# Splitting float64 weights with one ScalarE pass and no GpSimd work in a two-stage token network

## The chip, the core and the metric

The kernel runs on one core of a Trainium2 chip. Five engines take part, each with its own queue, worked off in order: TensorE (PE, with PEld for its weight loads), VectorE (DVE), ScalarE (ACT), GpSimd (POOL) and SyncE (SP), which issues most transfers. The metric is device time in microseconds (us) of one execution; the median of three timed executions of the kernel before is 1495.04 us (1490.94 to 1497.68).

## What is computed

The reference chains three parts. Only the last two carry float64 weights that the change touches.

```
x   = attention(q, k pooled by 8, v pooled by 8)          # 8 x 576 tokens, 512 wide
x   = moe(x)            # 8 experts, each token goes to one: relu(x @ w1[e]) @ w2[e], times a gate
h   = x @ w_in                                            # 4608 x 512 by 512 x 2048
g   = h * clip(h + 3, 0, 6) / 6
out = g @ w_out                                           # 4608 x 2048 by 2048 x 512
```

`w_in` and `w_out` come in as float64. The chip's engines work with 32 bits, so the kernel reads each float64 as two 32-bit words and makes two float32 numbers of it, a high part (what TensorE takes in its float32r format) and a low part (the rest). Activations are split into a high and a low part too. Each product is then three matmuls: high by high, low by high, high by low.

## The kernel before

It runs in three stages. **Attention** builds the tokens and writes them, ordered by expert, to memory. **moe1** works in units of 400 tokens of one expert; beside its matmuls each unit of its loop loads and splits a piece of `w_in` (two pieces of 128 by 416 values, by `conv` inside `moe1`, all on VectorE). **moe2** is the last stage: 9 blocks of 512 tokens, and in each block 16 steps, one for each 128 columns of the 2048 wide middle layer. Step s does

- `h_mm(s)`: 12 matmuls into `hps` (128 by 512); ScalarE makes r = relu(hps + 3); VectorE makes r = min(r, 6) * hps; ScalarE rounds it to `gh`; the low part is `gl` = r - gh.
- `o_mm(s - 2)`: 12 matmuls of `gh` and `gl` with the high and low part `wo` of one 128 by 512 tile of `w_out`, added up over the 16 steps in four PSUM tiles.

In the first block alone, step s begins with `conv(s)`, which makes the `wo` tiles of that step from the loaded tile `ds` (32-bit words, high and low word side by side), and then `conv_load(s + 2)` asks for the `ds` tile of the step after next. After steps 3, 6, 9 and 12 `y_split` also splits a tile of the next block's input: a copy on ScalarE (`yhl`, high) and a difference on VectorE (`yhl`, low). I call these four the split steps.

The order on TensorE, VectorE, ScalarE and SyncE is the order in which the code is written. On VectorE, step s of the first block is: the seven operations of `conv(s)` (lines 989 to 995), r (line 1016), and, in a split step, the low part of `yhl` (line 745). On ScalarE it is: the high part `wo[0]` (line 997, needs line 993), r (line 1015), `gh` (line 1019, needs line 1016), in a split step the high part of `yhl`. On GpSimd it is: the difference a - high (line 998), the sum that gives the low part `wo[1]` (line 999), and, in the first block alone, `gl` (line 1020); later blocks make `gl` on VectorE. TensorE cannot begin the matmuls of `o_mm(s)` with `wo[1]` before line 999 is done, nor those with `gl` before line 1020 is.

The seven VectorE operations of `conv` are: clear the sign of the high word (989), a floor (990), shift by 3 and mask (991), put the sign back (992), flip one exponent bit to get the float32 a (993), cut a's mantissa off to get a power of two, ex (994), low word times ex (995).

Of the kernel before, what the change touches and what calls it, by code (L numbers as in the profile page):

```python
# [8 lines left out]
F32 = mybir.dt.float32  # L9
F32R = mybir.dt.float32r  # L10
BF16 = mybir.dt.bfloat16
I32 = mybir.dt.int32
U32 = mybir.dt.uint32
AF = mybir.ActivationFunctionType
ALU = mybir.AluOpType
# [36 lines left out]
F64_MIN = 2.0 ** -15 * 1.125  # L52
# [6 lines left out]
def setup(tc, g, cp):  # L59
    nc = tc.nc  # L60
    g.idn = cp.tile([P, P], F32, name="idn")
    make_identity(nc, g.idn)
    g.three = cp.tile([P, 1], F32, name="three")
    nc.vector.memset(g.three, 3.0)
    g.sgn = cp.tile([P, 1], I32, name="sgn")
    nc.vector.memset(g.sgn, -2 ** 31)


def attention(tc, g, moe, ins, xr_d):
# [675 lines left out]
    nc.vector.tensor_tensor(lo, src, hi.bitcast(F32), op=ALU.subtract)  # L745


def moe1(tc, g, xr_d, tok_d, y_d, w1, w2, w_in):
    nc = tc.nc
    s = Ctx()  # L750
# [89 lines left out]
    def conv(t, c, h):  # L840
        sh = [P, 2, CW]
        hw = t[:, :, :, 1]
        u, a, m, ex = (s.cv.tile(sh, I32, name=n, tag=n) for n in ("u", "a", "m", "ex"))
        oh = g.wi[0][:, 2 * h:2 * h + 2, bass.ds(c, CW)]
        ol = g.wi[1][:, 2 * h:2 * h + 2, bass.ds(c, CW)]
        v = nc.vector
        af = a.bitcast(F32)
        return [
            lambda: v.tensor_scalar(u, hw, 0x7FFFFFFF, None, op0=ALU.bitwise_and),
            lambda: v.tensor_scalar(m.bitcast(F32), u.bitcast(F32), F64_MIN, None, op0=ALU.max),  # L850
            lambda: v.tensor_scalar(u, m, 3, 0x7FFFFFFF, op0=ALU.logical_shift_left, op1=ALU.bitwise_and),
            lambda: v.scalar_tensor_tensor(m, hw, g.sgn, u, op0=ALU.bitwise_and, op1=ALU.bitwise_or),
            lambda: v.tensor_scalar(a, m, 0x40000000, None, op0=ALU.bitwise_xor),
            lambda: v.tensor_scalar(ex, m, -0x800000, 0x40000000, op0=ALU.bitwise_and, op1=ALU.bitwise_xor),
            lambda: v.scalar_tensor_tensor(u.bitcast(F32), t[:, :, :, 0].bitcast(U32), 2.0 ** -52, ex.bitcast(F32),
                                           op0=ALU.mult, op1=ALU.mult),
            lambda: v.tensor_scalar(oh, af, 1.0, None, op0=ALU.mult),
            lambda: v.tensor_tensor(m.bitcast(F32), af, oh.bitcast(F32), op=ALU.subtract),
            lambda: v.tensor_tensor(ol, m.bitcast(F32), u.bitcast(F32), op=ALU.add),
        ]  # L860

    def unit(i, first=False, last=False, tail=None):
        e = s.e0 if first else reg(0, i, E - 1)
# [98 lines left out]
def moe2(tc, g, tok_d, y_d, w_out, out):  # L962
    nc = tc.nc
    es = ExitStack()
    pool = lambda n, b, **kw: es.enter_context(tc.tile_pool(name=n, bufs=b, reuse_waits="tile", **kw))
    c1 = pool("dc", 1)
    gp = pool("dg", 3)
    op = pool("do", 3)
    cv = pool("dcv", 1)
    ps_h = pool("ps_h", 3, space=PSUM)  # L970
    ps_o = pool("ps_o", 1, space=PSUM)
    NB = NT // 512
    KF = F2 // P
    wo = [[c1.tile([P, DM], F32R, name=f"wo{h}_{f}") for f in reversed(range(KF))][::-1] for h in (1, 0)][::-1]
    three, sgn = g.three, g.sgn
    yhl, y_load, y_split = g.yhl, g.y_load, g.y_split

    sts, conv_load = g.sts, g.wo_load

    def conv(f):  # L980
        s = sts.pop(f)
        sh = [P, DM]
        hw = s[:, :, 1]
        u = cv.tile(sh, I32, name="du", tag="u")
        a = cv.tile(sh, I32, name="da", tag="a")
        m = cv.tile(sh, I32, name="dm", tag="m")
        ex = cv.tile(sh, I32, name="dex", tag="ex")
        v = nc.vector
        v.tensor_scalar(u, hw, 0x7FFFFFFF, None, op0=ALU.bitwise_and)  # L989
        v.tensor_scalar(m.bitcast(F32), u.bitcast(F32), F64_MIN, None, op0=ALU.max)  # L990
        v.tensor_scalar(u, m, 3, 0x7FFFFFFF, op0=ALU.logical_shift_left, op1=ALU.bitwise_and)  # L991
        v.scalar_tensor_tensor(m, hw, sgn, u, op0=ALU.bitwise_and, op1=ALU.bitwise_or)  # L992
        v.tensor_scalar(a, m, 0x40000000, None, op0=ALU.bitwise_xor)  # L993
        v.tensor_scalar(ex, m, -0x800000, 0x40000000, op0=ALU.bitwise_and, op1=ALU.bitwise_xor)
        v.scalar_tensor_tensor(wo[1][f], s[:, :, 0].bitcast(U32), 2.0 ** -52, ex.bitcast(F32), op0=ALU.mult, op1=ALU.mult)
        af = a.bitcast(F32)
        nc.scalar.copy(wo[0][f], af)
        nc.gpsimd.tensor_tensor(ex.bitcast(F32), af, wo[0][f].bitcast(F32), op=ALU.subtract)
        nc.gpsimd.tensor_tensor(wo[1][f], ex.bitcast(F32), wo[1][f].bitcast(F32), op=ALU.add)  # L999

    tkf = c1.tile([P, NT // P], F32, name="tkf")
    tki = c1.tile([P, NT // P], I32, name="tki")
    gg = {}

    def h_mm(s):
        j, f = divmod(s, KF)
        yh, yl = yhl[j]
        ps = ps_h.tile([P, 512], F32, name="hps", tag="h")
        n = 0
        for k in range(4):  # L1010
            for a, b in ((0, yh), (0, yl), (1, yh)):
                nc.tensor.matmul(ps, g.wi[a][:, k, f * P:(f + 1) * P], b[:, k], start=(n == 0), stop=(n == 11))  # L1012
                n += 1
        r = gp.tile([P, 512], F32, name="r", tag="r", bufs=2)
        nc.scalar.activation(r, ps, AF.Relu, bias=three)  # L1015
        nc.vector.scalar_tensor_tensor(r, r, 6.0, ps, op0=ALU.min, op1=ALU.mult)  # L1016
        gh = gp.tile([P, 512], F32R, name="gh", tag="gh")
        gl = gp.tile([P, 512], F32R, name="gl", tag="gl")
        nc.scalar.copy(gh, r)  # L1019
        (nc.gpsimd if s < KF else nc.vector).tensor_tensor(gl, r, gh.bitcast(F32), op=ALU.subtract)  # L1020
        gg[s] = (gh, gl)

    pso = {}

    def put(j, t):
        o = op.tile([P, DM], F32, name="osb", tag="osb")
        if t % 2:
            nc.vector.tensor_scalar(o, pso[j][t], 1.0 / 6.0, None, op0=ALU.mult)
        else:
            nc.scalar.activation(o, pso[j][t], AF.Copy, scale=1.0 / 6.0)  # L1030
# [45 lines left out]
def chunk_kernel(ctx, tc, q, k, v, mid, w_gate, mbias, w1, w2, w_in, w_out, out):  # L1076
# [76 lines left out]
```

## Time and profile before

| | us |
|---|---|
| median of three timed runs | 1495.04 (1490.94 to 1497.68) |
| the profiled execution, its own time | 1481.43 |
| span of its trace, first to last instruction | 1479.7 |
| PE busy / DVE busy / ACT busy / POOL busy | 1426.0 / 793.7 / 533.6 / 259.3 |

The profile gives the busy time of each engine, the share of each in slices of the span, the chain of work that ended last, and groups of instructions. PE's busy share is high nearly everywhere, since its matmuls overlap and their ends are modelled, so whether it waits is read from the matmuls' idle times and from their count in a stretch. Attention takes the first 208 us, moe1 goes to 648.8 us of the trace, and moe2 fills the rest; its first block, in which the weights are split, lies between 649 and 767 us.

### The profile page before, as it was taken

How to read it: one execution, taken by the hardware profiler on the slowest of the kernel's cores; microseconds unless marked ns; L12 is line 12 of the kernel's file. 1: busy time of each engine (PE TensorE's matmuls, PEld its weight loads, DVE VectorE, ACT ScalarE, POOL GpSimd, SP SyncE). 2: the span in 40 equal slices, each digit the busy share in tenths (PEclk: the TensorE clock that was granted, in tenths of full speed). 3: DMA queues.
4: the chain of work that ended last, by engine and by line, in shares of the span. 5: the costliest groups of instructions: out<-in, count | busy, mean ns of one | idle time of the engine just before them, and what ended most of it. 6: DMA issues, size and time to landing. Idle time of an engine off the chain costs nothing.

```text
span 1479.7 us, 22270 instructions
## 1 busy us (share of the span) xinstructions
PE 1426.0 (96%) x7385; PEld 1243.1 (84%) x7385; DVE 793.7 (54%) x1554; ACT 533.6 (36%) x1057; POOL 259.3 (18%) x265
## 2 busy tenths in 40 slices
PE   7998989999999999998889999999999999999998
PEld 5787879999999999986668888888888888888886
DVE  7879875877777777668873232222223223232222
ACT  3556654444444444422232222222222222222222
POOL 5537231111111111025550010100001010010101
PEclk8999999999999999999999999999999999999999
DMA  8989155666666666452220010100101010000000
GB/s 271 295 282 325 67 167 177 203 190 186 190 186 187 195 186 191 130 145 78 86 86 15 15 38 20 36 15 8 43 15 36 15 36 15 15 29 0 29 1 29
DMA packets 128937, 156.57 MB, mean 106 GB/s; under 512 B 18466, under 2 KB 87074, under 8 KB 128866
## 3 DMA queue, kind: packets, MB, share of 16 engines
q1 hardware_dynamic: 123106, 135.54, 30.5%
q0 software_dynamic: 5760, 20.10, 3.6%
q8 instruction: 43, 0.70, 0.2%
q14 instruction: 28, 0.23, 0.1%
HBM read 118.26 MB, written 37.34 MB: 105 GB/s over the span
## 4 chain that ended last, share of the span: by engine, by line
issue 41%; PE 8%; DVE 6%; POOL 2%; ACT 1%; POOLq 0%; DVEq 0%; ACTq 0%
PE ops L1040 3%; PE hps L1012 3%; POOL out_dram L1031 2%; DVE dm L990 1%; PE ph L874 1%; DVE du L991 1%; PE y L887 1%; DVE du L989 1%; DVE dm L992 1%; ACT r L1015 1%; DVE r L1016 1%; DVE da L993 0%; DVE yhl L745 0%; ACT gh L1019 0%; ACT yhl L744 0%
## 5 line engine op out<-in xcount | busy, mean ns | idle before, releaser
L1012 PE MATMUL hps<-yhl,wi 128*128 128x512 f32 x1728 | 419.3, 391 | 0.0
L1012 PEld LDWEIGHTS hps<-yhl,wi 128*128 128x128 f32 x1728 | 325.3, 188 | 73.0
L1040 PE MATMUL ops<-wo,gh 128*128 128x512 f32 x1152 | 366.8, 398 | 3.4 <-POOL wo L999 3.4
L1016 DVE SCALAR_TENSOR_TENSOR r<-r,hps 128x512 f32<-128x512 f32 x144 | 98.9, 686 | 397.8 <-ACT r L1015 397.7
L1040 PEld LDWEIGHTS ops<-wo,gh 128*128 128x128 f32 x1152 | 217.7, 189 | 57.7 <-POOL wo L999 7.6
L1015 ACT ACTIVATE r<-hps,three 128x512 f32<-128x512 f32 x144 | 99.3, 690 | 415.6 <-PE hps L1012 415.0
L1040 PE MATMUL ops<-wo,gl 128*128 128x512 f32 x576 | 230.3, 400 | 12.8 <-POOL gl L1020 12.6
L745 DVE TENSOR_TENSOR wl<-ws,wh 128x512 fp32r<-128x512 f32 x192 | 136.2, 739 | 40.8 <-ACT wh L744 33.4
L744 ACT CAST wh<-ws 128x512 fp32r<-128x512 f32 x192 | 116.5, 619 | 106.3 <-PE y L887 55.4
L1031 POOL DMA_INDIRECT out_dram<-osb,tki x36 | 34.5, 959 | 674.6 <-ACT osb L1030 664.7
L1040 PEld LDWEIGHTS ops<-wo,gl 128*128 128x128 f32 x576 | 108.9, 189 | 43.0 <-POOL gl L1020 17.3
L1020 DVE TENSOR_TENSOR gl<-r,gh 128x512 fp32r<-128x512 f32 x128 | 88.9, 695 | 87.8 <-ACT gh L1019 87.8
L874 PE MATMUL ph<-xhi,wh 128*128 128x400 f32 x384 | 132.1, 344 | 2.2 <-PEq L1148 1.2
L887 PE MATMUL y<-hi,wh 128*128 128x400 f32 x384 | 133.9, 349 | 0.0
L887 PE MATMUL y<-lo,wh 128*128 128x400 f32 x384 | 132.4, 345 | 0.5 <-DVE lo L879 0.5
L874 PE MATMUL ph<-xlo,wh 128*128 128x400 f32 x384 | 132.6, 345 | 0.0
L874 PE MATMUL ph<-xhi,wl 128*128 128x400 f32 x384 | 132.6, 345 | 0.0
L887 PE MATMUL y<-hi,wl 128*128 128x400 f32 x384 | 131.4, 342 | 0.0
L1019 ACT CAST gh<-r 128x512 fp32r<-128x512 f32 x144 | 89.2, 620 | 109.7 <-DVE r L1016 109.7
L797 POOL TENSOR_TENSOR cxg<-cxg 100x512 f32<-100x512 f32 x48 | 57.7, 1205 | 331.4 <-PE ph L874 257.3
L878 ACT ACTIVATE hi<-ph 128x400 fp32r<-128x400 f32 x96 | 48.4, 504 | 106.4 <-PE ph L874 98.2
L879 DVE SCALAR_TENSOR_TENSOR lo<-ph,hi 128x400 fp32r<-128x400 f32 x96 | 54.9, 572 | 58.1 <-ACT hi L878 57.7
(194 smaller groups left out, 1692.0 us busy)
## 6 DMA issues: line engine op xcount, KB each, us to landing
ws<-in_moe_w_dram SPq DMA_DIRECT2D x192, 256.0 KB, 3.9
cxg<-xr SPq DMA_DIRECT2D x44, 225.8 KB
yd<-yo SPq DMA_DIRECT2D x12, 800.0 KB, 6.7
yt<-yd SPq DMA_DIRECT2D x36, 256.0 KB
cs<-in_moe_w_in_dram SPq DMA_DIRECT2D x20, 416.0 KB, 3.6
kv<-in_k_dram SPq DMA_DIRECT2D x16, 512.0 KB
kv<-in_v_dram SPq DMA_DIRECT2D x16, 512.0 KB
ds<-in_moe_w_out_dram SPq DMA_DIRECT2D x16, 512.0 KB
```

The source lines that it names most:

```text
L744: nc.scalar.copy(hi, src)
L745: nc.vector.tensor_tensor(lo, src, hi.bitcast(F32), op=ALU.subtract)
L797: nc.gpsimd.tensor_tensor(s.xg[:, t, 0:DM].rearrange("p (h x) -> p h x", x=D), v, s.xg[:, t, GC:GC + 1].unsqueeze(2).to_broadcast([T4, H, ...
L874: nc.tensor.matmul(ph, a[j][:, 0, k * P:(k + 1) * P], b[k], start=(n == 0), stop=(n == 11))
L887: nc.tensor.matmul(yps[d], a[j][:, 1, d * P:(d + 1) * P], b, start=(f == 0 and n == 0), stop=(f == 7 and n == 2))
L1012: nc.tensor.matmul(ps, g.wi[a][:, k, f * P:(f + 1) * P], b[:, k], start=(n == 0), stop=(n == 11))
L1015: nc.scalar.activation(r, ps, AF.Relu, bias=three)
L1016: nc.vector.scalar_tensor_tensor(r, r, 6.0, ps, op0=ALU.min, op1=ALU.mult)
L1019: nc.scalar.copy(gh, r)
L1020: (nc.gpsimd if s < KF else nc.vector).tensor_tensor(gl, r, gh.bitcast(F32), op=ALU.subtract)
L1031: i_ = nc.gpsimd.indirect_dma_start(out=out, out_offset=bass.IndirectOffsetOnAxis(ap=tki[:, 4 * j + t:4 * j + t + 1], axis=0), in_=o, in_o ...
L1040: nc.tensor.matmul(pso[j][t], a[:, t * P:(t + 1) * P], wo[b][f], start=(f == 0 and n == 0), stop=(f == KF - 1 and n == 2))
```

## The change

The split of a float64 tile becomes one function, `f64_ops`, used by both `conv` functions. It needs one operation less on integers: the sign is cleared by ScalarE's absolute value instead of a mask on VectorE, and the mask constant `sgn` now keeps the sign and one exponent bit, so that putting the sign back gives the float32 a at once and the bit flip goes away. In moe2 the two operations that GpSimd did (difference and sum) are VectorE's, and `gl` is VectorE's in the first block as in the others. In moe1 the high part stays on VectorE.

```diff
-    nc.vector.memset(g.sgn, -2 ** 31)
+    nc.vector.memset(g.sgn, -2 ** 30)

+def f64_ops(nc, g, hw, lw, a, m, ex, hi, lo, copy):
+    v = nc.vector
+    f = lambda t: t.bitcast(F32)
+    return [
+        lambda: nc.scalar.activation(f(ex), f(hw), AF.Abs),
+        lambda: v.tensor_scalar(f(m), f(ex), F64_MIN, None, op0=ALU.max),
+        lambda: v.tensor_scalar(m, m, 3, 0x3FFFFFFF, op0=ALU.logical_shift_left, op1=ALU.bitwise_and),
+        lambda: v.scalar_tensor_tensor(a, hw, g.sgn, m, op0=ALU.bitwise_and, op1=ALU.bitwise_or),
+        lambda: v.tensor_scalar(ex, a, -0x800000, None, op0=ALU.bitwise_and),
+        lambda: copy(hi, f(a)),
+        lambda: v.scalar_tensor_tensor(f(m), lw.bitcast(U32), 2.0 ** -52, f(ex), op0=ALU.mult, op1=ALU.mult),
+        lambda: v.tensor_tensor(f(ex), f(a), hi.bitcast(F32), op=ALU.subtract),
+        lambda: v.tensor_tensor(lo, f(ex), f(m), op=ALU.add),
+    ]
...
     def conv(f):
         s = sts.pop(f)
         sh = [P, DM]
         hw = s[:, :, 1]
...
-        v.scalar_tensor_tensor(wo[1][f], s[:, :, 0].bitcast(U32), 2.0 ** -52, ex.bitcast(F32), op0=ALU.mult, op1=ALU.mult)
-        af = a.bitcast(F32)
-        nc.scalar.copy(wo[0][f], af)
-        nc.gpsimd.tensor_tensor(ex.bitcast(F32), af, wo[0][f].bitcast(F32), op=ALU.subtract)
-        nc.gpsimd.tensor_tensor(wo[1][f], ex.bitcast(F32), wo[1][f].bitcast(F32), op=ALU.add)
+        a, m, ex = (cv.tile(sh, I32, name=f"d{n}", tag=n) for n in ("a", "m", "ex"))
+        for op_ in f64_ops(nc, g, hw, s[:, :, 0], a, m, ex, wo[0][f], wo[1][f], nc.scalar.copy):
+            op_()
...
-        (nc.gpsimd if s < KF else nc.vector).tensor_tensor(gl, r, gh.bitcast(F32), op=ALU.subtract)
+        nc.vector.tensor_tensor(gl, r, gh.bitcast(F32), op=ALU.subtract)
```

In `f64_ops` I name the operations by what they write, in order: abs, floor, shift, a, ex, high, m, difference, sum.

VectorE's queue in the first block of moe2, from r of step 3 to r of step 4, in the kernel before (`dm`, `da`, `dex`, `du` are the tiles m, a, ex and u of `conv`, and the brackets name the engines whose semaphores an instruction waits for):

```order
L1016 SCALAR_TENSOR_TENSOR r<-r,hps 128x512 [waits Activation_49]
L745 TENSOR_TENSOR yhl_4315<-yt,yhl_4314 128x512 [waits DMAHW0_49,Activation_49]
L989 TENSOR_SCALAR du<-ds 128x512 [waits DMAHW1_49]
L990 TENSOR_SCALAR dm<-du 128x512 [waits DVE_49]
L991 TENSOR_SCALAR du<-dm 128x512 [waits DVE_49]
L992 SCALAR_TENSOR_TENSOR dm<-ds,sgn,du 128x512 [waits DVE_49]
L993 TENSOR_SCALAR da<-dm 128x512 [waits DVE_49,Pool_49]
L994 TENSOR_SCALAR dex<-dm 128x512 [waits Pool_49]
L995 SCALAR_TENSOR_TENSOR wo_4_4128<-ds,dex 128x512 [waits DVE_49]
L1016 SCALAR_TENSOR_TENSOR r<-r,hps 128x512 [waits Activation_49]
```

The same stretch of VectorE's queue in the changed kernel:

```order
L1006 SCALAR_TENSOR_TENSOR r<-r,hps 128x512 [waits Activation_49]
L1010 TENSOR_TENSOR gl<-r,gh 128x512 [waits PE_49,Activation_49]
L745 TENSOR_TENSOR yhl_4303<-yt,yhl_4302 128x512 [waits DMAHW0_49,Activation_49]
L754 TENSOR_SCALAR dm<-dex 128x512 [waits Activation_49]
L755 TENSOR_SCALAR dm<-dm 128x512 [waits DVE_49]
L756 SCALAR_TENSOR_TENSOR da<-ds,sgn,dm 128x512 [waits DMAHW1_49,DVE_49]
L757 TENSOR_SCALAR dex<-da 128x512 [waits DVE_49]
L759 SCALAR_TENSOR_TENSOR dm<-ds,dex 128x512 [waits DVE_49]
L760 TENSOR_TENSOR dex<-da,wo_4_4140 128x512 [waits DVE_49,Activation_49]
L761 TENSOR_TENSOR wo_4_4124<-dex,dm 128x512 [waits DVE_49]
L1006 SCALAR_TENSOR_TENSOR r<-r,hps 128x512 [waits Activation_49]
```

`gl` now stands right behind r and waits for ScalarE's `gh`; the floor waits for ScalarE's abs; difference and sum stand ahead of r; two of the four one-input forms are gone.

ScalarE's queue at the same place before, from `gh` of step 3 to `gh` of step 4:

```order
L1019 CAST gh<-r 128x512 [waits DVE_49]
L744 CAST yhl_4314<-yt 128x512 [waits DMAHW0_49]
L997 CAST wo_4_4144<-da 128x512 [waits DVE_49]
L1015 ACTIVATE r<-hps,three 128x512 [waits PE_49,Pool_49]
L1019 CAST gh<-r 128x512 [waits DVE_49]
```

And now:

```order
L1009 CAST gh<-r 128x512 [waits DVE_49]
L744 CAST yhl_4302<-yt 128x512 [waits DMAHW0_49]
L753 ACTIVATE dex<-ds 128x512 [waits DMAHW1_49]
L758 CAST wo_4_4140<-da 128x512 [waits DVE_49]
L1005 ACTIVATE r<-hps,three 128x512 [waits PE_49,Activation_49]
L1009 CAST gh<-r 128x512 [waits DVE_49]
```

The abs of step 4 (line 753) stands behind `gh` and `yhl` of step 3 and ahead of the high part of step 4. On GpSimd the three operations of every step are gone and nothing takes their place.

## Rows read from the trace of the kernel before

**Rows 1.** Busy us (instructions) by stretch: PE, PEld, DVE, ACT, POOL; clock, DMA, GB/s.
```profile
400.00:620.00 220.00, 218.79 (x1255) 217.88 (x1254) 165.07 (x296) 95.53 (x183) 29.58 (x24) 1.00 0.61 182
649.00:767.00 118.00, 101.81 (x400) 76.18 (x400) 103.60 (x136) 33.59 (x56) 65.77 (x48) 0.97 0.29 88
767.00:1470.00 703.00, 703.00 (x3043) 571.68 (x3043) 202.13 (x299) 188.99 (x299) 31.12 (x33) 1.00 0.07 22
```

**Rows 2.** Waits from 649 to 767: who waited for whom, us, times, longest.
```profile
PE ops L1040 <- POOL gl L1020: 12.6, 13, 1.2
```

**Rows 3.** Matmuls on PE in time: start us, us, line, count, [idle before <-releaser].
```profile
657.46 0.40 PE L1040 MATMUL ops<-wo,gl 128*128 128x512 f32 x1
...
766.49 0.50 PE L1040 MATMUL ops<-wo,gl 128*128 128x512 f32 x1 [0.73 <-POOL gl L1020]
```

**Rows 4.** VectorE in time, one plain step of the first block.
```profile
748.63 0.69 DVE L1016 SCALAR_TENSOR_TENSOR r<-r,hps 128x512 f32<-128x512 f32 x1 [0.21 <-ACT r L1015]
749.23 0.92 DVE L989 TENSOR_SCALAR du<-ds 128x512 int32<-128x512 int32 x1
750.19 1.41 DVE L990 TENSOR_SCALAR dm<-du 128x512 f32<-128x512 f32 x1
751.63 1.37 DVE L991 TENSOR_SCALAR du<-dm 128x512 int32<-128x512 int32 x1
753.04 0.75 DVE L992 SCALAR_TENSOR_TENSOR dm<-ds,sgn,du 128x512 int32<-128x512 int32 x1
753.89 0.43 DVE L993 TENSOR_SCALAR da<-dm 128x512 int32<-128x512 int32 x1
754.24 0.42 DVE L994 TENSOR_SCALAR dex<-dm 128x512 int32<-128x512 int32 x1
754.69 0.70 DVE L995 SCALAR_TENSOR_TENSOR wo<-ds,dex 128x512 fp32r<-128x512 uint32 x1
755.60 0.69 DVE L1016 SCALAR_TENSOR_TENSOR r<-r,hps 128x512 f32<-128x512 f32 x1 [0.21 <-ACT r L1015]
```

**Rows 5.** VectorE in time, in a split step.
```profile
740.51 0.69 DVE L1016 SCALAR_TENSOR_TENSOR r<-r,hps 128x512 f32<-128x512 f32 x1 [0.21 <-ACT r L1015]
...
745.14 0.43 DVE L990 TENSOR_SCALAR dm<-du 128x512 f32<-128x512 f32 x1
745.61 0.43 DVE L991 TENSOR_SCALAR du<-dm 128x512 int32<-128x512 int32 x1
```

**Rows 6.** GpSimd in time: the step of rows 4, and its last operation of the block.
```profile
749.95 1.36 POOL L999 TENSOR_TENSOR wo<-dex,wo 128x512 fp32r<-128x512 f32 x1
751.27 1.45 POOL L1020 TENSOR_TENSOR gl<-r,gh 128x512 fp32r<-128x512 f32 x1
...
765.16 1.28 POOL L1020 TENSOR_TENSOR gl<-r,gh 128x512 fp32r<-128x512 f32 x1
```

**Rows 7.** VectorE and ScalarE in time, at the start of the block.
```profile
650.33 0.75 DVE L992 SCALAR_TENSOR_TENSOR dm<-ds,sgn,du 128x512 int32<-128x512 int32 x1
651.12 0.43 DVE L993 TENSOR_SCALAR da<-dm 128x512 int32<-128x512 int32 x1
...
652.82 0.69 DVE L1016 SCALAR_TENSOR_TENSOR r<-r,hps 128x512 f32<-128x512 f32 x1
...
649.01 0.49 ACT L943 COPY yo<-y 128x400 f32<-128x400 f32 x1 [0.60 <-PE y L887]
```

**Rows 8.** VectorE in time, in the second block, where it makes `gl` itself.
```profile
778.20 0.69 DVE L1016 SCALAR_TENSOR_TENSOR r<-r,hps 128x512 f32<-128x512 f32 x1 [3.35 <-ACT r L1015]
779.57 0.69 DVE L1020 TENSOR_TENSOR gl<-r,gh 128x512 fp32r<-128x512 f32 x1 [0.69 <-ACT gh L1019]
```

**Rows 9.** ScalarE in time, in the step of rows 4.
```profile
754.36 0.62 ACT L997 CAST wo<-da 128x512 fp32r<-128x512 f32 x1 [4.38 <-DVE da L993]
754.88 0.68 ACT L1015 ACTIVATE r<-hps,three 128x512 f32<-128x512 f32 x1
756.32 0.62 ACT L1019 CAST gh<-r 128x512 fp32r<-128x512 f32 x1 [0.75 <-DVE r L1016]
```

More of the change, by code (lines that the diff above doesn't have):

```diff
@@ L842, in conv @@
         hw = t[:, :, :, 1]
-        u, a, m, ex = (s.cv.tile(sh, I32, name=n, tag=n) for n in ("u", "a", "m", "ex"))
+        a, m, ex = (s.cv.tile(sh, I32, name=n, tag=n) for n in ("a", "m", "ex"))
         oh = g.wi[0][:, 2 * h:2 * h + 2, bass.ds(c, CW)]
         ol = g.wi[1][:, 2 * h:2 * h + 2, bass.ds(c, CW)]
-        v = nc.vector
-        af = a.bitcast(F32)
[L848 to L860, printed above, removed]
+        return f64_ops(nc, g, hw, t[:, :, :, 0], a, m, ex, oh, ol, lambda o, i_: nc.vector.tensor_scalar(o, i_, 1.0, None, op0=ALU.mult))
     def unit(i, first=False, last=False, tail=None):
@@ L974, in moe2 @@
     wo = [[c1.tile([P, DM], F32R, name=f"wo{h}_{f}") for f in reversed(range(KF))][::-1] for h in (1, 0)][::-1]
-    three, sgn = g.three, g.sgn
+    three = g.three
     yhl, y_load, y_split = g.yhl, g.y_load, g.y_split
@@ L983, in conv @@
         hw = s[:, :, 1]
[L984 to L994, printed above, removed]
-        v.scalar_tensor_tensor(wo[1][f], s[:, :, 0].bitcast(U32), 2.0 ** -52, ex.bitcast(F32), op0=ALU.mult, op1=ALU.mult)
-        af = a.bitcast(F32)
-        nc.scalar.copy(wo[0][f], af)
-        nc.gpsimd.tensor_tensor(ex.bitcast(F32), af, wo[0][f].bitcast(F32), op=ALU.subtract)
-        nc.gpsimd.tensor_tensor(wo[1][f], ex.bitcast(F32), wo[1][f].bitcast(F32), op=ALU.add)
+        a, m, ex = (cv.tile(sh, I32, name=f"d{n}", tag=n) for n in ("a", "m", "ex"))
+        for op_ in f64_ops(nc, g, hw, s[:, :, 0], a, m, ex, wo[0][f], wo[1][f], nc.scalar.copy):
+            op_()
     tkf = c1.tile([P, NT // P], F32, name="tkf")
```

## The prediction

> **What bounds the kernel now.** I read the busy times by stretch first [rows 1]. In moe1, 400 to 620 us, TensorE works 218.79 of 220 us, so nothing that the change does there can gain over about 1 us in 220. In moe2 behind its first block, 767 to 1470 us, it works all of 703 us: 3043 matmuls, 0.231 us each, so a step of 24 matmuls lasts 24 x 0.231 = 5.54 us and TensorE sets the time. In between, 649 to 767 us, TensorE runs only 400 matmuls in 118 us, while VectorE is busy 103.6 us. The waits of that stretch [rows 2] say for whom TensorE stands still: for `gl` from GpSimd, 13 times. How much could be had is seen on TensorE itself [rows 3]: from the first matmul with `gl` of step 0 at 657.46 to that of step 15 at 766.49 it spends 109.0 us on 15 steps, which at 5.54 us would be 83.1. So 25.9 us is the ceiling of any cure of this block.
>
> What sets the block's pace is VectorE [rows 4]: in a plain step its operations follow each other nearly without a gap, from r at 748.63 to r at 755.60, 6.97 us. In a split step it is 8.12 us (740.51 to 748.63) [rows 4, 5]. Of 15 intervals 4 are split ones. GpSimd's three operations start when VectorE's and ScalarE's results let them, and they slow VectorE: the floor (990) takes 1.41 us and the shift (991) 1.37 us [rows 4] just while GpSimd runs lines 999 and 1020, 749.95 to 752.72 [rows 6], whereas two forms of the same kind behind that, 993 and 994, take 0.43 and 0.42 us, and in a split step, after GpSimd is done, the floor and the shift take 0.43 us each [rows 5].
>
> **The change in moe2's first block.** GpSimd does nothing there any more, so I cost every VectorE operation by rows without GpSimd, from start to start: floor to shift 0.47 [rows 5]; shift to a the same form, 0.47; a to ex 0.79 (650.33 to 651.12) [rows 7]; ex to m 0.45 (754.24 to 754.69) [rows 4]. The difference now waits for two semaphores, VectorE's own and ScalarE's; before, line 993 did so and began 0.10 us behind the end of the operation ahead (753.04 + 0.75 to 753.89) [rows 4], so m to difference is 0.70 + 0.10 = 0.80. Difference to sum: 0.69 + 0.04 = 0.73, by the gap behind 992 [rows 7]. Sum to r, which waits for nothing on VectorE: 0.60 (748.63 to 749.23) [rows 4]. Then the new wait: `gl` needs ScalarE's `gh`, which needs r. The second block has this already: 1.37 us from r to `gl` [rows 8]. Behind it stand the floor of the next step, and through it the whole next step. `gl` to floor: 0.60. The sum is 0.47 + 0.47 + 0.79 + 0.45 + 0.80 + 0.73 + 0.60 + 1.37 + 0.60 = **6.28 us** a plain step, and 0.60 more, **6.88**, a split one. That is still over TensorE's 5.54, so VectorE keeps the block, with 0.7 us of waiting a step on TensorE in place of 1.4.
>
> ScalarE's new abs lies beside it. `gh` starts 0.72 us after r, the next operation of ScalarE 0.52 later, and a 128x512 copy takes 0.62 [rows 9]; the abs thus ends 1.86 us behind r, and the floor, in VectorE's own order, starts at 1.37 + 0.60 = 1.97. It fits with 0.07 us to spare after a hand-over of 0.04. ScalarE has room: it waited 4.38 us for a in that step [rows 9]. The high part starts when a is done and ends 0.66 later, while VectorE does ex and m for 1.25; relu for r ends 1.24 behind a and is wanted at about 2.6. Both are covered by VectorE's own work; without it, each would cost at most its 0.6 to 0.7 us.
>
> The abs reads every second word of `ds`, and no row shows ScalarE reading so. I bound it by 0.62 us (shorter gains nothing, `gl` is then the later one) and by double, 1.24; I take 0.62, since on VectorE the form that reads `ds` with the same stride, 992, shows no doubling (0.75 us) [rows 4]. Doubled, a plain step grows by 0.55, a split one by 0.47 and the start by 0.62: 11 x 0.55 + 4 x 0.47 + 0.62 = 8.6 us in all. The Trainium skill, page "SBUF — State Buffer", section "SBUF: two separate sides", says that consecutive accesses to one 16-byte line go at full speed, so that a stride of up to four 32-bit words is free; by it the abs is not doubled and the sum stays. No run here shows that.
>
> The sum for the block: ScalarE's last copy of moe1 ends at 649.50 [rows 7], the first abs at 650.12, the floor starts at 650.16, r of step 0 comes 4.31 us later (the chain without its last two terms) at 654.47, against 652.82 before [rows 7]: 1.65 us lost. Then 11 x 6.28 + 4 x 6.88 = 96.6 us, 0.60 for one small conversion (line 1066) that both kernels have in the block, and 1.37 + 0.69 for the last `gl`: it ends at **753.7 us**. Before, GpSimd's last one ended at 765.16 + 1.28 = 766.44 [rows 6]. From there on TensorE runs without a pause in either kernel, so the gain is **12.7 us**. If the double wait of the difference costs nothing (0.60 in place of 0.80, the nearest row without a wait), it is 15.7; if a to ex also costs a double wait (0.85), 11.8.
>
> A rule speaks against moving the sign mask. The Trainium skill, page "ScalarE: Activation LUTs", section "Rules for kernel authors", wants simple elementwise work on VectorE, not on ScalarE, as VectorE is quicker for each element. The rows agree on the speed (0.62 us against 0.43), but not on the cost: ScalarE waits 4.38 us a step, VectorE does not, so keeping the mask on VectorE would cost 0.47 us on each of 16 steps, 7.5 us, and the sum by the rule would be 5.2 us gained.
>
> **The rest.** Transfers: SyncE's load of `ds` for step s + 2 now waits for abs and m of step s; the next load of `yt` stands behind it. m is done some 3 us into the step and the data is wanted two steps on, so over 9 us cover it; I put it at nothing. In moe1 each of 20 pieces moves one operation to ScalarE, takes one more off VectorE and makes VectorE wait for ScalarE. ScalarE is busy 95.5 of 220 us there and TensorE has no gap [rows 1], so I put it at nothing, between a gain of 1 us and a loss, if each abs held TensorE for its full 0.5 us (0.62 x 416/512), of 20 x 0.5 = 10 us.
>
> **Rivals.**
> 1. *The abs is slow for its stride.* 1.24 us, as above, leaves 12.7 - 8.6 = 4 us: 1491. For it: no margin but 0.07 us. Against it: VectorE's strided form.
> 2. *VectorE is quicker than the rows that I added up, and TensorE takes the block over.* Then the ceiling holds, 25.9 us: 1469. For it: three terms rest on a wait whose price I take from one row. Against it: 0.74 us a step would have to go, and only 0.20 of it is doubtful.
> 3. *The slow forms stay slow, and the kernel gets slower.* If floor and shift are slow for another reason than GpSimd, they keep 1.44 and 1.41 us from start to start [rows 4]: 0.97 + 0.94 = 1.91 us a step, 15 x 1.91 = 28.7, less the 12.7 gained: 16 us slower, 1511. It decides from 0.85 us a step on for both together (12.7 / 15). For it: they are slow in most steps. Against it: the quick ones of the split step, and lines 993 and 994 [rows 4, 5]. The Trainium skill, page "SBUF — State Buffer", section "Who interferes with whom", says that such VectorE forms and a GpSimd operation shut each other out for the whole of an instruction. By that rule the rival falls; this trace agrees, with 1.41 us under GpSimd and 0.43 without.
> 4. *The change gains nothing that can be told*, since moe1 gives it back through waits on abs: up to 10 us, 1492.
>
> **How the numbers follow.** The profiled execution took 1481.43 us; 12.7 less is 1468.7. The median of the timed runs is 13.6 us above the profiled one; the block's gain does not depend on that, so I take it off the median: 1495.04 - 12.7 = **1482.3**. The forecast, a gain of 8 to 18 us, has 0.72; rival 1 has 0.10, rival 2 has 0.07, rival 3 has 0.05, rival 4 has 0.06. About 0.5%, 7.5 us, is what a measurement of this kernel can tell from no change. Faster by more: 0.72 + 0.07 + 0.03 (a milder rival 1) = 0.82. Within: 0.07 + 0.05 = 0.12. Slower: 0.06. The range takes in both bounds of the terms, most of rivals 1 and 4 and the spread of the runs, about 3 us to each side: 1475 to 1491.
>
> **What would show it.** The step from r to r on VectorE at 6.28 us and 6.88; floor and shift at 0.43 in every step; abs at 0.62 and the floor following `gl` without a wait on ScalarE; 1.37 from r to `gl`; TensorE waiting for VectorE's `gl` about 0.7 us a step; the last `gl` 12 to 13 us earlier; moe1 as long as before. An abs of over 0.7 us, a floor over 0.5, or TensorE waits in moe1 would prove me wrong.

## The result, and the profile after

The changed kernel takes **1475.86 us** (median of four runs, 1472.28 to 1479.97) against 1493.49 for the kernel before (four runs, 1490.94 to 1497.68): a ratio of 0.9899, interval 0.9876 to 0.9921. In a second comparison with more runs (`after_again`, below) the ratio is 0.9929, 0.9908 to 0.9949. The profiled execution took 1472.28 us, its span is 1470.2 us. The forecast was 1482.3 in 1475 to 1491: the direction and the size hold, and the median lies 0.9 us above the range's low end. 1 - 13.3 / 1493 = 0.991 lies in both intervals, and 13.3 us is what the first block of moe2 gained. One of the ten executions of `e1_gl_only` below took 2329.05 us at a mean granted clock of 0.557, where all others of this document lie between 0.97 and 0.99; it stands in none of the numbers.

The first two views are the busy times of the whole page, and those of two of the stretches of [rows 1] (columns as there):

```profile
PE 1422.6 (97%) x7385; PEld 1237.2 (84%) x7385; DVE 757.7 (52%) x1530; ACT 551.9 (38%) x1093; POOL 191.3 (13%) x217
```

```profile
400.00:620.00 220.00, 218.79 (x1255) 217.89 (x1254) 155.38 (x277) 102.44 (x199) 27.43 (x24) 1.00 0.62 182
649.00:767.00 118.00, 112.54 (x461) 83.73 (x460) 94.62 (x161) 46.27 (x79) 3.89 (x4) 1.00 0.31 97
```

In moe1 TensorE is as busy as before, 218.79 of 220 us, while 9.7 us of VectorE's work are gone and 6.9 us of ScalarE's have come. In the window of the block TensorE gets 461 matmuls done where it had done 400, and GpSimd has 3.89 us left of 65.77; in the changed kernel this window also takes in some 10 us behind the block.

VectorE in time, the first plain step, a split step, and the last `gl` of the block (they answer to [rows 4, 5, 7]):

```profile
657.86 0.68 DVE L1006 SCALAR_TENSOR_TENSOR r<-r,hps 128x512 f32<-128x512 f32 x1
659.23 0.69 DVE L1010 TENSOR_TENSOR gl<-r,gh 128x512 fp32r<-128x512 f32 x1 [0.69 <-ACT gh L1009]
659.84 0.42 DVE L754 TENSOR_SCALAR dm<-dex 128x512 f32<-128x512 f32 x1
660.29 0.43 DVE L755 TENSOR_SCALAR dm<-dm 128x512 int32<-128x512 int32 x1
660.75 0.75 DVE L756 SCALAR_TENSOR_TENSOR da<-ds,sgn,dm 128x512 int32<-128x512 int32 x1
661.54 0.43 DVE L757 TENSOR_SCALAR dex<-da 128x512 int32<-128x512 int32 x1
662.00 0.69 DVE L759 SCALAR_TENSOR_TENSOR dm<-ds,dex 128x512 f32<-128x512 uint32 x1
662.79 0.69 DVE L760 TENSOR_TENSOR dex<-da,wo 128x512 f32<-128x512 f32 x1
663.52 0.69 DVE L761 TENSOR_TENSOR wo<-dex,dm 128x512 fp32r<-128x512 f32 x1
664.13 0.68 DVE L1006 SCALAR_TENSOR_TENSOR r<-r,hps 128x512 f32<-128x512 f32 x1
...
676.68 0.68 DVE L1006 SCALAR_TENSOR_TENSOR r<-r,hps 128x512 f32<-128x512 f32 x1
...
678.65 0.68 DVE L745 TENSOR_TENSOR yhl<-yt,yhl 128x512 fp32r<-128x512 f32 x1
...
683.55 0.68 DVE L1006 SCALAR_TENSOR_TENSOR r<-r,hps 128x512 f32<-128x512 f32 x1
...
755.81 0.69 DVE L1010 TENSOR_TENSOR gl<-r,gh 128x512 fp32r<-128x512 f32 x1 [0.69 <-ACT gh L1009]
```

Read the starts: floor 659.84, shift 660.29, a 660.75, ex 661.54, m 662.00, difference 662.79, sum 663.52, r 664.13. From r to r it is 6.27 us in a plain step and 6.87 in a split one (676.68 to 683.55). The floor and the shift take 0.42 and 0.43 us in this step, and 0.42 or 0.43 in all 16. The only stretch of over 0.1 us in which VectorE stands still is the 0.69 us ahead of `gl`.

ScalarE in the same step ([rows 9] before):

```profile
658.57 0.62 ACT L1009 CAST gh<-r 128x512 fp32r<-128x512 f32 x1 [2.17 <-DVE r L1006]
659.10 0.67 ACT L753 ACTIVATE dex<-ds 128x512 f32<-128x512 f32 x1
661.54 0.62 ACT L758 CAST wo<-da 128x512 fp32r<-128x512 f32 x1 [1.77 <-DVE da L756]
662.06 0.68 ACT L1005 ACTIVATE r<-hps,three 128x512 f32<-128x512 f32 x1
```

The abs ends at 659.77 and the floor starts at 659.84 without a wait.

TensorE's waits from 640 to 770 us (who waited for whom: us in total, times, longest), and its first matmuls with `gl` of steps 0 and 15 ([rows 2, 3] before); PEld is TensorE's loading of weights, PE its matmuls:

```profile
PEld ops L1030 <- ACT gh L1009: 11.2, 14, 1.2
PEld ops L1030 <- DVE gl L1010: 6.0, 14, 0.4
PE ops L1030 <- ACT gh L1009: 5.3, 14, 0.8
```

```profile
660.85 0.40 PE L1030 MATMUL ops<-wo,gl 128*128 128x512 f32 x1
...
756.56 0.50 PE L1030 MATMUL ops<-wo,gl 128*128 128x512 f32 x1
```

From the first matmul with `gl` of step 0 to that of step 15 it is 756.56 - 660.85 = 95.71 us, 109.03 before [rows 3]: **13.3 us less**. What its matmuls still wait for is named `gh`, ScalarE's copy, and no longer `gl`; of its weight loads' waiting `gl` has 6.0 us and `gh` 11.2.

### The profile page after: what moved, and what is told of

Same layout as the page of the kernel before. It is cut to its first block, busy times and chain, and to the rows that moved or that the text cites. A ratio compares the mean times of both kernels' runs of the same rounds, so it can differ in the third digit from the quotient of the medians.

```text
span 1470.2 us, 22288 instructions
## 1 busy us (share of the span) xinstructions
PE 1422.6 (97%) x7385; PEld 1237.2 (84%) x7385; DVE 757.7 (52%) x1530; ACT 551.9 (38%) x1093; POOL 191.3 (13%) x217
## 4 chain that ended last, share of the span: by engine, by line
issue 47%; DVE 4%; PE 2%; POOL 2%; ACT 2%; POOLq 0%; DVEq 0%
POOL out_dram L1021 2%; PE ph L877 1%; PE y L890 1%; DVE da L756 1%; DVE r L1006 1%; ACT gh L1009 1%; DVE dex L760 1%; ACT r L1005 1%; DVE gl L1010 1%; DVE dm L755 0%; DVE dm L754 0%; DVE yhl L745 0%; DVE wo L761 0%; POOLq L1138 0%; ACT wo L758 0%
## 5 line engine op out<-in xcount | busy, mean ns | idle before, releaser
L1030 PEld LDWEIGHTS ops<-wo,gh 128*128 128x128 f32 x1152 | 215.3, 188 | 60.1 <-ACT gh L1009 11.2
L1010 DVE TENSOR_TENSOR gl<-r,gh 128x512 fp32r<-128x512 f32 x144 | 99.7, 692 | 98.8 <-ACT gh L1009 98.8
```

What stands on the lines that cost most here:

```text
L1010: nc.vector.tensor_tensor(gl, r, gh.bitcast(F32), op=ALU.subtract)
```

## The experiments

Each kernel was run beside the kernel before on the same chip, in three groups on three chips (medians before of 1490.35, 1486.26 and 1486.85 us); across groups only the ratios can be compared. The table has what their traces show of the block: r to r on VectorE in a plain and in a split step; from TensorE's first hps matmul to the end of the last `gl`, which the expectations call the block; and TensorE's 15 steps, counted as above. The column behind is the ratio that the 15 steps alone would give (their difference to 109.03, over the median before). Then the measured ratio with its interval. "moe1 from" is the start of moe1's first matmul in that trace, and the last column how long moe1 lasts, up to the first hps matmul.

| kernel | plain, split | block | 15 steps of TensorE | ratio by these | measured ratio | moe1 from | moe1 |
|---|---|---|---|---|---|---|---|
| before | 6.98, 8.11 | 117.6 | 109.03 | | | 208.4 | 440.4 |
| after | 6.27, 6.87 | 104.3 | 95.71 | 0.991 | 0.9899 [0.9876, 0.9921] | 211.4 | 440.8 |
| after_again | 6.27, 6.88 | 104.3 | 95.73 | 0.991 | 0.9929 [0.9908, 0.9949] | 216.1 | 441.0 |
| e1_gl_only | 7.03, 7.63 | 115.1 | 106.53 | 0.998 | 0.9981 [0.9960, 1.0003] | 210.1 | 440.3 |
| e2_sub_sum_only | 6.72, 8.24 | 115.0 | 106.38 | 0.998 | 0.9982 [0.9963, 1.0000] | 217.3 | 440.3 |
| e3_mask_on_vector | 6.73, 7.33 | 110.5 | 101.92 | 0.995 | 0.9965 [0.9953, 0.9977] | 214.7 | 441.0 |
| e4_moe2_only | 6.27, 6.87 | 104.3 | 95.69 | 0.991 | 0.9907 [0.9884, 0.9929] | 217.0 | 440.9 |
| e5_gpsimd_back | 9.2, 10.0 | 149.3 | 141.02 | 1.022 | 1.0244 [1.0200, 1.0287] | 217.0 | 440.6 |
| e6_no_second_wait | 6.07, 6.68 | 101.1 | 92.56 | 0.989 | 0.9884 [0.9833, 0.9935] | 207.7 | 440.3 |
| e7_early_alone | 5.37, 5.97 | 90.9 | 83.20 | 0.983 | 0.9822 [0.9802, 0.9842] | 210.2 | 440.3 |
| e8_early_both | 5.18, 5.78 | 87.7 | 83.20 | 0.983 | 0.9842 [0.9822, 0.9862] | 218.7 | 441.4 |

Every ratio that the block alone gives lies in the measured interval, but for e3's, which misses it by 0.0001. So of what is measured nothing has to be sought outside this block: in all of these kernels the time changes with TensorE's 15 steps in it.

**after_again: the changed kernel once more, beside the other experiments.** No edit.

> The changed kernel as it is. Theory (all of the gain lies in moe2's first block, 13.3 us there in its trace): ratio to before 0.991, moe1 440 us from its first to its last matmul as before, first block 104 us from the first matmul of moe2 to the end of the last gl of the block, before 117.6. Rival (a further 3 to 5 us come from elsewhere, since the first runs gave 17.6 us): ratio 0.988 and moe1 or the attention stage shorter in the trace.

1478.61 us (six runs) against 1490.35 (17 runs). The block is the same to 0.02 us, but moe1 starts 4.7 us later than in the first trace, at 216.1 us. For one and the same kernel, that is the spread of the attention stage, whose code the change does not touch; over all twelve traces it is 207.7 to 218.7 us.

**e4_moe2_only: moe1's conversion as before, moe2's as changed.** Against the changed kernel:

```diff
 def conv(...):           # moe1
-    a, m, ex = ...       # f64_ops: nine operations, the first on ScalarE
+    u, a, m, ex = ...    # the ten operations of before, mask on VectorE
```

> The changed kernel with moe1's split as before (ten operations, all on VectorE), so that only moe2 is changed. Theory (moe1 is bound by TensorE): as the changed kernel, ratio 0.991, block 104 us, moe1 440 us. Rival (moe1's shorter split or its new wait counts): moe1 differs from the changed kernel's by over 1 us.

1476.43 us against 1490.35, a ratio of 0.9907 beside 0.9929 of `after_again`, with intervals that overlap. moe1 takes 440.9 us with the old conversion and 440.8 and 441.0 with the new one. The change in moe1 is worth nothing that shows, in either direction, as [rows 1] let one expect: TensorE has no gap there that a shorter VectorE could close. Rival 4 is out.

**e5_gpsimd_back: GpSimd busy again, with operations that nobody waits for.** Against the changed kernel, ahead of `gl`; the three results are never read:

```diff
+if s < KF:
+    x = cv.tile([P, 512], F32, name="x", tag="x")
+    for _ in range(3):
+        nc.gpsimd.tensor_tensor(x, r, gh.bitcast(F32), op=ALU.subtract)
 nc.vector.tensor_tensor(gl, r, gh.bitcast(F32), op=ALU.subtract)
```

> The changed kernel with GpSimd working again beside it: three differences of r and gh into a tile that nobody reads, in each step of the first block, as long as the three operations that the change took away; the output is not changed by them. Theory (GpSimd's work slows VectorE's forms): floor and shift, or the operations next to them, take 0.9 to 1.5 us, over 7.5 us a step, block over 122 us, ratio over 1.0. Rival (VectorE is quicker only since it has other operations): 6.27 us a step, block 104 us, ratio 0.991.

1523.96 us against 1486.26, 2.4% slower than before. VectorE and GpSimd in time, one plain step:

```profile
711.52 0.69 DVE L1014 TENSOR_TENSOR gl<-r,gh 128x512 fp32r<-128x512 f32 x1 [0.68 <-ACT gh L1009]
712.13 1.51 DVE L754 TENSOR_SCALAR dm<-dex 128x512 f32<-128x512 f32 x1
713.67 1.40 DVE L755 TENSOR_SCALAR dm<-dm 128x512 int32<-128x512 int32 x1
715.10 1.66 DVE L756 SCALAR_TENSOR_TENSOR da<-ds,sgn,dm 128x512 int32<-128x512 int32 x1
716.80 0.43 DVE L757 TENSOR_SCALAR dex<-da 128x512 int32<-128x512 int32 x1
...
711.63 4.60 POOL L1013 TENSOR_TENSOR x<-r,gh 128x512 f32<-128x512 f32 x3 [4.65 <-ACT gh L1009]
```

From 711.63 to 716.23 GpSimd works, and the three VectorE operations that start in that time take 1.51, 1.40 and 1.66 us where they took 0.42, 0.43 and 0.75. The one behind is quick again. The instructions of VectorE are those of the changed kernel, so what slows floor and shift is GpSimd, and rival 3 (slow for another reason) is out. The Trainium skill, page "SBUF — State Buffer", section "Who interferes with whom", says that such VectorE forms and a GpSimd instruction that reads SBUF block each other for a whole instruction rather than slow each other down. This trace agrees: an operation of 0.42 us takes 1.51, about as long as one of GpSimd's three, 4.60 / 3 = 1.53 us.

**e1_gl_only and e2_sub_sum_only: one half of GpSimd's work moved at a time.** Against the kernel before:

```diff
 # e1
-(nc.gpsimd if s < KF else nc.vector).tensor_tensor(gl, r, gh.bitcast(F32), op=ALU.subtract)
+nc.vector.tensor_tensor(gl, r, gh.bitcast(F32), op=ALU.subtract)
 # e2
-nc.gpsimd.tensor_tensor(ex.bitcast(F32), af, wo[0][f]..., op=ALU.subtract)
-nc.gpsimd.tensor_tensor(wo[1][f], ex.bitcast(F32), ...)
+v.tensor_tensor(...)      # both, on VectorE
```

> The kernel before with one part of the change: gl of the first block on VectorE; difference and sum stay on GpSimd. Theory (GpSimd's operations slow VectorE's by holding them off, so taking one away gives back more than gl and its wait cost): floor and shift at 0.43 us, since GpSimd is done by then, gl at up to 1.3; about 6.6 us a plain step, first block 110 to 113 us, ratio 0.996. Rival (only the number of operations on VectorE counts): 6.97 + 1.37 = 8.3 us a step, block about 138 us, ratio 1.013.

> The kernel before with another part of the change: difference and sum of moe2 on VectorE, gl of the first block on GpSimd, the old integer operations. Theory (GpSimd's holding off): one GpSimd operation a step is left, behind gh, and it holds off one of VectorE's forms for about 1 us; 6.6 us a plain step, block 109 to 114 us, ratio 0.995. Rival (the number of operations counts): 6.97 + 0.73 + 0.60 = 8.3 us a step, block about 138 us, ratio 1.013.

1484.40 (nine executions) and 1483.30 us against 1486.26: each alone gains 2.5 and 2.7 us of TensorE's 15 steps, and neither can be told from no change. Both were expected to gain more: a block of 110 to 113 and of 109 to 114 us, where 115.1 and 115.0 came. e1, VectorE and GpSimd in time:

```profile
713.22 1.81 DVE L1020 TENSOR_TENSOR gl<-r,gh 128x512 fp32r<-128x512 f32 x1 [0.69 <-ACT gh L1019]
...
715.48 0.43 DVE L990 TENSOR_SCALAR dm<-du 128x512 f32<-128x512 f32 x1
...
713.18 1.30 POOL L999 TENSOR_TENSOR wo<-dex,wo 128x512 fp32r<-128x512 f32 x1
```

e2, the same view, a split step and the start of the next:

```profile
706.67 1.35 DVE L745 TENSOR_TENSOR yhl<-yt,yhl 128x512 fp32r<-128x512 f32 x1 [1.21 <-ACT yhl L744]
...
714.55 1.46 DVE L991 TENSOR_SCALAR du<-dm 128x512 int32<-128x512 int32 x1
716.04 0.75 DVE L992 SCALAR_TENSOR_TENSOR dm<-ds,sgn,du 128x512 int32<-128x512 int32 x1
...
706.19 1.28 POOL L1020 TENSOR_TENSOR gl<-r,gh 128x512 fp32r<-128x512 f32 x1 [5.44 <-ACT gh L1019]
714.44 1.28 POOL L1020 TENSOR_TENSOR gl<-r,gh 128x512 fp32r<-128x512 f32 x1 [6.97 <-ACT gh L1019]
```

In e1 the floor is quick (0.43 us), but now `gl` starts 0.04 us behind GpSimd's line 999 and takes 1.81 us: it ends 0.55 us behind it. In e2 GpSimd's only operation still catches the shift (1.46 us), and in a split step the low part of `yhl` (1.35 us). The hold moves to whichever VectorE operation begins while GpSimd works; I had priced each operation by the place in which it met GpSimd before. The two gains add up to 5.2 of the 13.3 us, but the rest is not what both halves together would give. The changed kernel has one thing more: of VectorE's five one-input operations of `conv` (989, 990, 991, 993 and 994 in its queue, where I had counted four) two are gone, the mask and the bit flip. No run leaves GpSimd idle and keeps these two. An estimate from e2's trace: with `gl` on VectorE as well, the hold of the shift goes (716.04 - 714.55 = 1.49 us to the next operation, 0.46 without) and from r to the next step's first operation it is 1.37 + 0.61 in place of 0.60. That makes 6.72 - 1.03 + 1.38 = 7.07 us a plain step, 7.68 a split one, against 6.98 and 8.11 before, and a block of about 116 us for 117.6. By this estimate the three operations that VectorE takes over from GpSimd cost nearly all that the end of the holding gives back, and most of the 13.3 us is the shorter chain: 6.2 us for the mask (e3, below) and, by difference, some 5 for the flip. Whether the shorter chain would gain as much beside GpSimd's work, no run shows.

**e3_mask_on_vector: the changed kernel with the mask on VectorE.**

```diff
-lambda: nc.scalar.activation(f(ex), f(hw), AF.Abs),
+lambda: v.tensor_scalar(ex, hw, 0x7FFFFFFF, None, op0=ALU.bitwise_and),
```

> The changed kernel with the sign cleared by a mask on VectorE, as before, in place of ScalarE's abs, in moe1 and moe2. Theory (VectorE sets the block's pace and ScalarE's time is free): 0.46 us more a step, 6.73 plain and 7.33 split, block 110 to 111 us, ratio 0.995. Rival (the abs costs on ScalarE what it saves on VectorE, by the Trainium skill, page ScalarE: Activation LUTs, section Rules for kernel authors, which wants such work on VectorE): block at most 104 us, ratio at most 0.991.

1485.31 us against 1490.35. VectorE in time:

```profile
709.02 0.68 DVE L1006 SCALAR_TENSOR_TENSOR r<-r,hps 128x512 f32<-128x512 f32 x1
...
711.00 0.42 DVE L753 TENSOR_SCALAR dex<-ds 128x512 int32<-128x512 int32 x1
...
715.75 0.68 DVE L1006 SCALAR_TENSOR_TENSOR r<-r,hps 128x512 f32<-128x512 f32 x1
```

The mask adds 0.46 us to the step (6.73 for 6.27), and to the block 6.2 us, as the chain of VectorE says. GpSimd is idle here too, and TensorE's 15 steps gain 7.1 us of the 13.3. The rule of the Trainium skill, page "ScalarE: Activation LUTs", section "Rules for kernel authors", by which simple elementwise work (`relu`, `max`, `min`, `add`, `mul`) belongs on VectorE, would cost these 6.2 us here: VectorE's 0.42 us lie on the chain, ScalarE's 0.67 us do not.

**e6_no_second_wait: the difference no longer waits for the product.** In the changed kernel it writes over ex, which m reads, and so waits for VectorE's own m beside ScalarE's high part. Here the product goes into `wo[1]` and the difference into m's tile, and ScalarE's high part is its only wait:

```diff
-v.scalar_tensor_tensor(f(m), lw..., f(ex), ...)    # m
-v.tensor_tensor(f(ex), f(a), hi..., subtract)      # difference
-v.tensor_tensor(lo, f(ex), f(m), add)              # sum
+v.scalar_tensor_tensor(lo, lw..., f(ex), ...)
+v.tensor_tensor(f(m), f(a), hi..., subtract)
+v.tensor_tensor(lo, f(m), lo.bitcast(F32), add)
```

> The changed kernel with m written to the low part's tile and the difference to m's, so that the difference waits for ScalarE alone. Theory (the second wait costs 0.20 us, 0.80 against 0.60 from m to difference): 6.07 us a plain step, block 101 us, ratio 0.989. Rival (the price of 0.80 lies in the operation, not in the wait): block 104 us as the changed kernel.

1466.74 us against 1486.26. VectorE in time, m and difference:

```profile
714.17 0.69 DVE L759 SCALAR_TENSOR_TENSOR wo<-ds,dex 128x512 fp32r<-128x512 uint32 x1
714.78 0.68 DVE L760 TENSOR_TENSOR dm<-da,wo 128x512 f32<-128x512 f32 x1
```

From m to difference it is 0.61 us where the changed kernel has 0.79. Over 16 steps 0.2 us make 3.2, which is what the block is shorter by (101.1 for 104.3).

**e7_early_alone: floor and shift of the next step stand between `gh` and `gl`.** The abs of step s + 1 is issued ahead of step s's r, its floor and shift run while ScalarE copies `gh`; tile ex gets a second buffer for that. The edit, shortened:

```diff
-conv(s)
-h_mm(s)
+for op_ in ops[3:]: op_()         # a ... sum of step s
+ops = conv(s + 1); ops[0]()       # abs of the next step
+h_mm(s, ops[1:3])                 # floor and shift of the next step
 ...
 nc.scalar.copy(gh, r)
+for op_ in mid: op_()
 nc.vector.tensor_tensor(gl, r, gh.bitcast(F32), op=ALU.subtract)
```

> The changed kernel with the order of e8_early_both (abs, floor and shift of the next step ahead of gl), but with the difference's second wait left in. Theory (the wait for gh is 0.77 us of VectorE's step, the second wait 0.20): 5.4 to 5.5 us a plain step and 6.0 to 6.1 a split one on VectorE, 5.6 on the mean, just over TensorE's 5.54; from the first matmul with gl of step 0 to that of step 15 84 to 86 us, ratio 0.984 to 0.986. Rival (the gain of e8_early_both came from the second wait): 89 us or more, ratio 0.988.

**1459.81 us** (1457.54 to 1461.77) against 1486.85: 27 us less than before and the lowest ratio of all, though e6's and e8's intervals overlap with its own. VectorE in time, then TensorE in time at the same step:

```profile
705.93 0.68 DVE L1004 SCALAR_TENSOR_TENSOR r<-r,hps 128x512 f32<-128x512 f32 x1
706.53 0.42 DVE L754 TENSOR_SCALAR dm<-dex 128x512 f32<-128x512 f32 x1
706.98 0.43 DVE L755 TENSOR_SCALAR dm<-dm 128x512 int32<-128x512 int32 x1
707.32 0.69 DVE L1010 TENSOR_TENSOR gl<-r,gh 128x512 fp32r<-128x512 f32 x1
```

```profile
703.08 0.63 PE L1030 MATMUL ops<-wo,gh 128*128 128x512 f32 x2
...
708.63 0.63 PE L1030 MATMUL ops<-wo,gh 128*128 128x512 f32 x2
```

`gl` starts 1.39 us behind r, as late as before the edit, but the 0.69 us of waiting ahead of it are gone: two operations that stood behind `gl` stand there now. VectorE's plain step is 5.37 us, under TensorE's 5.55 (708.63 - 703.08), and TensorE waits for nothing in the whole block. Expected were 84 to 86 us with VectorE just over TensorE; with its split steps of 5.97 VectorE needs 5.54 on the mean, and TensorE's own pace sets the 83.20.

**e8_early_both: e7 and e6 together.**

> The changed kernel with VectorE's and ScalarE's order moved: abs of the next step behind the high part, floor and shift of the next step between r and gl, so that they fill the wait for gh; and the product m written to the low part's tile, so that the difference has no second wait. Theory (VectorE's chain of 6.28 us a step is the bound, and 0.77 of it is the wait for gh, 0.20 the double wait): 5.2 to 5.3 us a plain step on VectorE, so TensorE takes over at 5.54; from the first matmul with gl of step 0 to that of step 15 83 to 86 us, 12 us less than the changed kernel, ratio 0.983. Rival (GpSimd's part was all of the gain and VectorE's waits cost nothing): as the changed kernel, 0.991.

1466.41 us against 1490.35. VectorE needs only 5.18 us a step and is done with its last `gl` 3.2 us sooner than in e7 (87.7 for 90.9), but TensorE's 15 steps take the same 83.20 us: 15 x 5.547, its own pace. What e6 saved by itself is worth nothing here. The intervals of e7 and e8 overlap, and the ratio that the block gives, 0.983, lies in both.

**e9_abs_adjacent: the abs reads words that lie side by side.** It reads a tile of the activation instead of every second word of `ds`, which makes the weights others than the input's. The edit, shortened (in the kernel the tile comes in as an argument):

```diff
-lambda: nc.scalar.activation(f(ex), f(hw), AF.Abs),
+lambda: nc.scalar.activation(f(ex), yhl[0][0][:, f % 4].bitcast(F32), AF.Abs),
```

> The changed kernel with moe2's abs reading 512 adjacent words of another tile in place of every second word of ds, so the weights of moe2 are not those of the input. Theory (ScalarE's 0.67 us for the abs, where a copy takes 0.62, comes from its form and not from the stride): abs still 0.67 us, step 6.27. Rival (the stride costs): abs 0.62 us, step 6.27 all the same, since gl is the later one.

1476.37 us (one run) beside 1486.85. ScalarE in time:

```profile
702.03 0.63 ACT L753 ACTIVATE dex<-yhl 128x512 f32<-128x512 f32 x1
```

0.63 us for 0.67: the few hundredths by which the abs is longer than a copy come from what it reads, by the edit the stride, and not, as the theory had it, from the form. The step stays at 6.27 us and TensorE's 15 steps at 95.67. The Trainium skill, page "SBUF — State Buffer", section "SBUF: two separate sides", calls a stride of up to four 32-bit words free; here a stride of two costs 0.04 us in 0.63, far from a doubling.

## Why the prediction was right, point by point

**VectorE sets the block's pace, and by its own chain.** Right. The nine pitches that were added up from rows of before came out within 0.02 us each: 1.37 from r to `gl`, then 0.61, 0.45, 0.46, 0.79, 0.46, 0.79, 0.73, 0.61, in all 6.27 us for the forecast 6.28, and 6.87 for 6.88. e3, e6 and e7 each changed one of these terms, and the block followed by that term times the steps, until TensorE took over.

**The start.** Right: r of step 0 was to come 5.65 us behind the first hps matmul, and came 657.86 - 652.2 = 5.66 behind it. That is 1.65 us later than before, the price of chaining the abs and the whole split ahead of the first r.

**The gain in the block, 12.7 us.** 13.3 measured, and the 0.6 us sit in one term. The 15 steps take 754.45 - 657.86 = 96.59 us from first to last r; 11 x 6.28 + 4 x 6.88 + 0.60 made 97.2. The term that was mis-sized is the 0.60 for the small conversion. VectorE in time, before and then after:

```profile
711.94 0.69 DVE L1066 CAST tki<-tkf 128x36 int32<-128x36 f32 x1
```

```profile
711.23 0.18 DVE L1056 CAST tki<-tkf 128x36 int32<-128x36 f32 x1
711.31 0.42 DVE L754 TENSOR_SCALAR dm<-dex 128x512 f32<-128x512 f32 x1
```

I took its price from the trace of before, where it ran beside GpSimd's line 998, though I costed all its neighbours by rows without GpSimd. Without GpSimd it is 0.18 us long, and the floor behind it comes 0.09 later than in another step. That is 0.5 of the 0.6 us. Even before, the step with it was only 0.13 us longer than a plain one (7.11 for 6.98).

**The abs beside `gl`.** Right, but closer than thought. It takes 0.67 us and not 0.62, so that of the margin of 0.07 us some 0.02 are left; the floor still follows `gl` without a wait. e9 shows that more margin would gain nothing. Rival 1, a doubled abs, is out.

**Rival 2, TensorE takes the block over.** Not in the changed kernel: VectorE's 6.27 stays over 5.55. The price that I had in doubt, the second semaphore of the difference, is 0.2 us (e6): the 0.60 that stood as the other bound to 0.80 is what a difference without that wait takes. The wait falls into 16 steps and not 15, so the bound named for it was 0.2 low: 12.7 + 3.2 = 15.9 for 15.7. The ceiling of this rival, 25.9 us, is right: e7 and e8 reach it, 109.03 - 83.20 = 25.8.

**What TensorE waits for.** Half wrong. The size was given as 0.7 us a step: (95.71 - 83.20) / 15 = 0.83 is measured, with the split steps in it. But it was to be `gl`, and most of it is `gh`: 5.3 us of the matmuls' waiting and 11.2 of the weight loads' are put down to ScalarE's copy, 6.0 to `gl`. The step asks for `gh` first, and r, from which both come, is what is late; `gl` follows by its own 0.69 us. I read the name over from [rows 2], where GpSimd made `gl` last and by itself.

**The mask by the rule.** Keeping it on VectorE was priced at 16 x 0.47 = 7.5 us. e3 measured 6.2: 15 steps of 0.46, less 0.69 us, since without the abs ahead of it the first r comes 4.97 us behind the first hps matmul and not 5.66. The sum by the rule, a gain of 5.2 us, is 7.1.

**moe1 for nothing.** Right, by e4.

**The number.** The gain of 12.7 us was taken off the median. The block gives 13.3, the medians 17.6 and 11.7. The profiled executions show how that comes about: the spans differ by 1479.7 - 1470.2 = 9.5 us, of which the block is 13.3 gained, while in the trace of after moe1 begins 3.0 us later and lasts 0.4 longer, and what follows the block is 0.4 longer. The start of moe1, anywhere between 207.7 and 218.7 us in these traces, varies by more than the forecast is off by. So the last `gl` ends only 766.44 - 756.50 = 9.9 us earlier, not the 12 to 13 that I named: I should have given that time from the block's first matmul on. For the same reason I do not explain the 4 us between the first measured gain and the block's. Of the 6.4 us by which the median lies under 1482.3, 0.6 are the conversion, 1.5 come from a median before of 1493.49 in place of 1495.04, and these 4 are the rest: that the median stayed inside the range, by 0.9 us, is in part luck.

## What to carry to other kernels

Where two engines hold each other off, look at what remains of the one that is relieved: with half of GpSimd's work moved (2.5 and 2.7 us) the hold only shifted to the next operation. And count what the moved work costs the engine that takes it over: by the estimate under e1 and e2 that was nearly all of the hold, and the gain came with the two operations that its chain lost, one of them to a ScalarE that had time. Price an operation that moves by rows in which its new neighbours run, and do so for the small ones too. And when a hand-over to another engine and back becomes a wait on the chain, put work of the next step into it: two operations placed there gained 12.5 us (e7), nearly as much as the change itself, up to the pace of the next engine, behind which a shorter chain is worth nothing (e8).

## What the runs showed of the hardware

A conversion of 36 words in a row is held like an operation on 512: 0.69 us beside GpSimd's operation, against 0.18 alone. GpSimd in the kernel before:

```profile
711.29 1.29 POOL L998 TENSOR_TENSOR dex<-da,wo 128x512 f32<-128x512 f32 x1 [3.20 <-ACT r L1015]
```

The hold ends with GpSimd's operation, and the held one then takes nearly its own time: it ends 0.05 us behind GpSimd's for this conversion (712.63 and 712.58; 0.18 us alone), 0.29 for the shift of e2 (716.01 and 715.72; 0.43 alone) and 0.55 for `gl` of e1 (715.03 and 714.48; 0.69 alone).

A wait for the VectorE operation just ahead costs time of its own: from m to difference 0.79 us with it and ScalarE's, 0.61 with ScalarE's alone (e6), and 0.73 from difference to sum with it alone.

TensorE's granted clock fell twice in the block of the kernel before and not in the changed one. TensorE before, by stretches of 4 us (busy us and matmuls, granted clock, DMA share, GB/s):

```profile
704.00:708.00 4.00, 2.40 (x10) 1.00 0.57 197
708.00:712.00 4.00, 3.85 (x10) 0.57 0.01 2
...
728.00:732.00 4.00, 2.24 (x9) 1.00 0.43 170
732.00:736.00 4.00, 4.00 (x12) 0.57 0.38 123
```

Both times the stretch ahead is one in which TensorE worked 2.40 and 2.24 of 4 us; but it worked 2.42 from 684 to 688 us too, and the clock stayed at 1.00 behind it, so these rows give no rule. 0.57 lies near the lower of its two levels, 1.2 of 2.4 GHz. An hps matmul in these stretches takes up to 632 ns in place of 389. It cost little: VectorE set the pace, and its steps about the second stretch, r at 726.55, 733.53 and 740.51, are the usual 6.98 us. About the first one step is 0.34 us longer, by a wait ahead of line 993 whose cause no run shows.
